# Adding the two halves of an attention output ahead of its transpose, and loading a head pair one step earlier

## The chip, the cores and the metric

The kernel runs on one core of one Trainium2 chip. The metric is the device time of one execution in microseconds (us). The engines of the core are TensorE (PE in the profile; its weight loads are listed apart as PEld), VectorE (DVE), ScalarE (ACT), GpSimd (POOL) and SyncE (SP, which only issues transfers here). They run side by side and each takes its own instructions strictly in order.

## The reference

Three blocks follow one another: attention in which a query sees only the keys that belong to the same of 16 clusters, a mixing layer with a two-layer ReLU network, and a gated network with a convolution of width 3. The change lies in the first block.

```python
def _attn_ref(q, k, v, centroids):          # q, k, v: 2 x 8 x 768 x 64
    ...
    q_assign = np.argmax(np.einsum('bhsd,hcd->bhsc', q_n, c_n), axis=-1)
    k_assign = np.argmax(np.einsum('bhsd,hcd->bhsc', k_n, c_n), axis=-1)
    mask = q_assign[:, :, :, None] == k_assign[:, :, None, :]
    scores = scale * np.matmul(q, k.transpose(0, 1, 3, 2))
    scores = np.where(mask, scores, -1000000000.0)
    scores = scores - np.max(scores, axis=-1, keepdims=True)
    attn = np.exp(scores)
    attn = attn / (np.sum(attn, axis=-1, keepdims=True) + 1e-09)
    return np.matmul(attn, v).astype(np.float32)
```

## The kernel before

Products are made with split operands: a number is kept as a high part, rounded to the format in which TensorE takes it fast, and a low part, the rest. So many tiles come in pairs (`ph`, `pl`; `wh`, `wl`), and the low part is a subtraction on VectorE or GpSimd.

**Tiles and stages of attention.** There are 2 batches of 8 heads; the heads go in 8 pairs, numbered 0 to 7. A head's 768 queries are 6 tiles of 128, so a pair has 12 steps (`s` = 0 to 11) and attention 96 (`n`). The function `step(n)` writes out by hand what each engine does in what order; three tiles of queries are one half of a head, numbered `g`. Within `step(n)` stand, in this order:

- `s_mm(n + 2)`: the scores `sc` of the tile two steps on, two products over `ab` and two over `cd` (which carries the cluster mask), into one of two score buffers.
- `pv_mm(g, r)`: four products of the transposed weights `ph` and `pl` with the values `vt`. After three steps the accumulator `pv` holds, for 384 queries, 64 rows of output from the values' high part and, in the other 64 partitions, 64 rows from their low part.
- `fin_t(g - 1)` (lines 340 to 345, in steps 1, 4, 7 and 10): three transposes of the finished half, `at`.
- `sims` of the next pair, in step 2: 12 small products that give the cluster similarities `sim`.
- `t_mm(n)`: six transposes `tr` of the exponentials, in two halves of three.
- `t_hi(n - 1)` on ScalarE and `t_lo(n - 1)` on VectorE: `ph` and `pl` from `tr`.
- `s_exp(n + 1)` on ScalarE, the exponential `e`, and `s_max(n + 2)` on VectorE, the row maximum of the next scores.
- `fin_a(g)` (lines 335 to 338, in steps 0, 3, 6 and 9): ScalarE copies the accumulator to `asb`, which frees it for the next half's `pv`.
- `fin_x(g - 1)` (lines 347 to 361, in the steps of `fin_t`): ScalarE copies `at` to `ats`, GpSimd adds the two 64-column halves and multiplies each of the three tiles by the reciprocal row sum `rs` into the result `X`.
- `prep(n)` (lines 543 to 575): work for the next pair. `load_raw` asks for the rows `rq` and `rk` on SP's queue, `load_ops` for the operands `ab` and `cd` of one head on GpSimd's queue, `split_ops` makes two subtractions on GpSimd from them, `load_v` the values; VectorE builds the one-hot cluster rows (`mx`, `eq`, `m`, `oh`) from `sim` in steps 2 to 5, TensorE transposes them (`oht`) in step 7, ScalarE makes `os` of them and SP writes them into `cd`. Every second step also moves a job on that fetches and splits weights of the later blocks (`wb`, `wx`, `wh`, `wl`).

**Buffers.** The accumulator `pv` has one buffer. `tr`, `at`, `sim`, `oht` and the later `mt`, `mu` share the three buffers of `ps_t`; a buffer is free when its reader on ScalarE or VectorE is done. `asb` and `ats` have one buffer each, `rq` and `rk` two, `ab` and `cd` three. After the last pair of attention its outputs are mixed (`mt`, in step 8 of the pair behind, needs `X`), and the two networks follow; nothing in them is touched.

## Time and profile before

| | before |
|---|---|
| median of 3 runs | 689.21 us (688.1 to 692.93) |
| the profiled execution | 691.09 us |
| its span, first to last instruction | 689.3 us |
| mean granted TensorE clock in it | 0.988 |
| attention in it | up to about 290 us |

A profile is one execution, recorded engine by engine. A row of a timeline gives the start in us from the span's start, how long the instruction or the run of like instructions took, engine, line of the kernel, operation, and the tiles as out<-in with partitions x elements; in brackets stands how long the engine was idle just before and whose completion ended that. The chain of work is followed back from the last instruction, at each step to what released it: it shows which engine set the pace, and where.

### The profile page before, as it was taken

To read this page: it belongs to the slowest core of one execution; us is meant where nothing else is said; L and a number is where in the kernel's file an instruction comes from. 1 tells how busy PE (TensorE), PEld (TensorE's weight loads), DVE (VectorE), ACT (ScalarE), POOL (GpSimd) and SP (SyncE) were. 2 spreads that over 40 slices of the span, in tenths; PEclk is the share of its full clock that TensorE was granted. 3 is DMA by queue.
4 is the path that set the end of the run, shared out by engine and by line. 5 is a ranking of instruction groups with operands and counts; after the bars stand their busy time and mean duration, and the time that the engine had idled before them with its cause. 6 is when DMAs were issued, how large, how long until landed. Compare 5 with 4: busy or idle time off the path is not lost.

```text
span 689.3 us, 10463 instructions
## 1 busy us (share of the span) xinstructions
PE 673.5 (98%) x3782; PEld 590.9 (86%) x3782; DVE 444.4 (64%) x825; ACT 372.9 (54%) x744; POOL 300.9 (44%) x391
## 2 busy tenths in 40 slices
PE   8799999999999999999999999999999999999997
PEld 6599899899999998888888888888887788888886
DVE  3688888887988898758731877775247535543400
ACT  3588879787878898424311343332133357753611
POOL 6747666666767632515530333332024643322300
PEclk7799999999999999999999999999999999999999
DMA  8957776776756510202310343442014000000111
GB/s 187 146 124 142 156 146 182 132 180 107 180 93 150 103 63 31 92 32 86 94 37 1 125 137 127 131 140 75 1 45 132 7 0 1 1 32 15 40 53 47
DMA packets 31827, 61.58 MB, mean 89 GB/s; under 512 B 15808, under 2 KB 19008, under 8 KB 31776
## 3 DMA queue, kind: packets, MB, share of 16 engines
q1 hardware_dynamic: 15632, 40.08, 19.3%
q0 software_dynamic: 16144, 20.84, 17.1%
q8 instruction: 30, 0.49, 0.3%
q14 instruction: 21, 0.17, 0.1%
HBM read 56.29 MB, written 3.15 MB: 86 GB/s over the span
## 4 chain that ended last, share of the span: by engine, by line
PE 81%; DVE 10%; ACT 2%; issue 2%; DMA 2%; POOL 1%; SPq 1%; ACTq 0%; DVEq 0%; POOLq 0%
PE g L764 10%; PE pv L328 8%; PE tr L304 7%; PE h L641 6%; PE h L643 6%; PE h L642 6%; PE a L657 5%; PE a L659 5%; PE a L658 5%; PE sc L266 4%; PE sc L277 4%; PE sim L203 3%; PE po L798 3%; PE po L799 3%; PE po L800 3%; DVE pl L317 2%
## 5 line engine op out<-in xcount | busy, mean ns | idle before, releaser
L442 POOL TENSOR_TENSOR wl<-wx,wh 128x512 fp32r<-128x512 f32 x48 | 63.1, 1317 | 113.8 <-ACT wh L441 113.4
L317 DVE TENSOR_TENSOR pl<-tr,ph 128x384 fp32r<-128x384 f32 x192 | 97.8, 549 | 22.4 <-ACT ph L313 21.8
L313 ACT CAST ph<-tr 128x384 fp32r<-128x384 f32 x192 | 83.7, 486 | 24.3 <-PE tr L304 23.7
L283 DVE TENSOR_SCALAR_CACHE_REDUCE e<-sc 128x768 f32<-128x768 f32 x96 | 90.8, 947 | 1.9 <-PE sc L277 1.9
L646 ACT ACTIVATE rh<-h 128x512 fp32r<-128x512 f32 (+1 forms) x52 | 29.3, 564 | 112.0 <-PE h L643 112.0
L295 ACT ACTIVATE e<-sc,nb 128x768 f32<-128x768 f32 x96 | 88.2, 919 | 3.0 <-DVE e L283 2.8
L304 PE MATMUL tr<-identf,e 128*128 128x128 f32 x576 | 84.4, 279 | 4.7 <-DVE pl L317 3.1
L647 DVE SCALAR_TENSOR_TENSOR rl<-h,rh 128x512 fp32r<-128x512 f32 (+1 forms) x52 | 33.7, 648 | 83.2 <-ACT rh L646 83.2
L641 PE MATMUL h<-uh,wh 128*128 128x512 f32 (+1 forms) x208 | 78.1, 376 | 1.6 <-DVE rl L647 1.6
L304 PEld LDWEIGHTS tr<-identf,e 128*128 128x128 f32 x576 | 67.5, 143 | 13.1 <-DVE pl L317 8.3
L657 PE MATMUL a<-rh,wh 128*128 128x512 f32 (+1 forms) x208 | 78.1, 375 | 0.5 <-DVE xa L673 0.5
L658 PE MATMUL a<-rl,wh 128*128 128x512 f32 (+1 forms) x208 | 77.7, 373 | 0.3 <-DVE rl L647 0.3
L659 PE MATMUL a<-rh,wl 128*128 128x512 f32 (+1 forms) x208 | 77.6, 373 | 0.0
L643 PE MATMUL h<-uh,wl 128*128 128x512 f32 (+1 forms) x208 | 77.6, 373 | 0.0
L642 PE MATMUL h<-ul,wh 128*128 128x512 f32 (+1 forms) x208 | 77.6, 373 | 0.0
L328 PE MATMUL pv<-ph,vt 128*128 128x384 f32 x192 | 66.0, 344 | 0.2 <-ACT asb L337 0.2
L328 PE MATMUL pv<-pl,vt 128*128 128x384 f32 x192 | 65.3, 340 | 0.0
L266 PE MATMUL sc<-ab 128*128 128x384 f32 x192 | 58.8, 389 | 2.6 <-ACT e L295 2.1
L441 ACT CAST wh<-wx 128x512 fp32r<-128x512 f32 x48 | 29.8, 620 | 57.6 <-DVE wx L395 57.5
L781 POOL TENSOR_TENSOR h<-h,cv 128x768 f32<-128x768 f32 x16 | 29.6, 1850 | 65.4 <-ACT cv L780 65.4
L391 DVE SCALAR_TENSOR_TENSOR wx<-wb,wx 128x512 int32<-128x512 int32 (+3 forms) x52 | 47.9, 920 | 11.3 <-ACT wb L382 9.3
L277 PE MATMUL sc<-cd 80*128 80x384 f32 x192 | 49.9, 342 | 0.5 <-DVE cd L240 0.5
(129 smaller groups left out, 1468.0 us busy)
## 6 DMA issues: line engine op xcount, KB each, us to landing
raw<-in_w_dram SPq DMA_DIRECT2D x32, 512.0 KB, 3.7
ab<-in_qk_dram POOLq DMA_DIRECT2D x30, 384.0 KB, 5.3
cd<-in_qk_dram POOLq DMA_DIRECT2D x15, 384.0 KB, 6.8
raw<-in_win_dram SPq DMA_DIRECT2D x8, 512.0 KB, 3.7
raw<-in_wout_dram SPq DMA_DIRECT2D x8, 512.0 KB, 3.7
rq<-in_qk_dram SPq DMA_DIRECT2D x8, 384.0 KB, 3.9
rk<-in_qk_dram SPq DMA_DIRECT2D x16, 192.0 KB, 4.4
rv<-in_vv_dram SPq DMA_DIRECT2D x8, 384.0 KB, 5.1
```

Source lines behind the costliest of these rows:

```text
L266: nc.tensor.matmul(ps[:, f, 0:HS], ab[:, 0, c0:c0 + P], ab[:, 1, f * HS:(f + 1) * HS], start=True, stop=False)
L283: nc.vector.tensor_scalar(out=e, in0=ps[:, :, 0:HS], scalar1=-SCALE, scalar2=3e38, op0=ALU.mult, op1=ALU.min, accum_out=nb,)
L295: nc.scalar.activation(e, ps[:, :, 0:HS], AF.Exp, scale=SCALE, bias=nb, accum_out=st["sum", n // 3][:, n % 3:n % 3 + 1])
L304: nc.tensor.transpose(pt[:, k, :], e[:, i, k * P:(k + 1) * P], identf)
L317: nc.vector.tensor_sub(lo, st.pop(("t", n, i)), hi)
L328: nc.tensor.matmul(acc, vt[:, h % 2, k, :], m[:, k].rearrange("p a b -> p (a b)"), start=(k == 0 and i == 0), stop=(k == NT - 1 and i == 1),)
L641: nc.tensor.matmul(ph, wh[:, k, ws], uh[g][:, k, ts], start=(k == 0), stop=False)
L642: nc.tensor.matmul(ph, wh[:, k, ws], ul[g][:, k, ts], start=False, stop=False)
L643: nc.tensor.matmul(ph, wl[:, k, ws], uh[g][:, k, ts], start=False, stop=(k == ND - 1))
L657: nc.tensor.matmul(accs[d][:, 0:n], wh[:, i, ds_], rh, start=(f == 0), stop=False)
L658: nc.tensor.matmul(accs[d][:, 0:n], wh[:, i, ds_], rl, start=False, stop=False)
L659: nc.tensor.matmul(accs[d][:, 0:n], wl[:, i, ds_], rh, start=False, stop=(f == NH - 1))
```

## The change

Four things are done.

1. `fin_a` no longer copies the whole accumulator. Each head has its own 64 partitions of a tile `xm` (0 to 63 for the even head of a pair, 64 to 127 for the odd one). ScalarE copies those of the accumulator there as they lie, and the accumulator's other 64 partitions, shifted by 64, into the same partitions of a tile `xo`; GpSimd adds the two in `xm`. `xm` has one tile for each half of the queries, `xo` is one tile.
2. `fin_t` transposes only behind odd heads, when both heads lie in `xm`: three transposes serve two heads. They stand behind the step's `tr` transposes now, and no longer ahead of them.
3. `fin_x` writes the reciprocals of an even head and leaves; behind an odd head it copies `at` to `ats` and makes one product for three tiles and two heads into `X`.
4. `load_raw` of the pair after next and `load_ops` of its first head are called in step 10 of the current pair, where before they were called in step 0 of the next one. Only the first pair ahead is left as it was. `split_ops` of the first head goes from step 2 to step 1, that of the second head from step 5 to step 7.

```diff
@@ -332,33 +332,48 @@
         if part == 2:
             st.pop(("pt", g))
 
+
+
+    xm = {}
+
     def fin_a(g):
-        asb = a_e.tile([P, HS], F32, tag="asb", name="asb", bufs=1)
-        nc.scalar.copy(asb, st.pop(("pv", g)))
-        st["asb", g] = asb
+        _, h, t0 = head_of(3 * g)
+        j, half = h % 2, t0 // 3
+        if j == 0:
+            xm[half] = a_e.tile([P, HS], F32, tag=f"xm{half}", name="xm", bufs=1)
+        x = xm[half][j * D:(j + 1) * D]
+        other = a_e.tile([P, HS], F32, tag="xo", name="xo", bufs=1)[j * D:(j + 1) * D]
+        acc = st.pop(("pv", g))
+        nc.scalar.copy(x, acc[j * D:(j + 1) * D])
+        nc.scalar.copy(other, acc[(1 - j) * D:(2 - j) * D])
+        nc.gpsimd.tensor_add(x, x, other)
 
     def fin_t(g):
-        asb = st.pop(("asb", g))
+        _, h, t0 = head_of(3 * g)
+        if h % 2 == 0:
+            return
         pt = ps_t.tile([P, 3, 2, D], F32, tag="t", name="at")
         for t in range(3):
-            nc.tensor.transpose(pt[:, t].rearrange("p a d -> p (a d)"), asb[:, t * P:(t + 1) * P], identf)
+            nc.tensor.transpose(pt[:, t].rearrange("p a d -> p (a d)"), xm[t0 // 3][:, t * P:(t + 1) * P], identf)
         st["at", g] = pt
 
     def fin_x(g):
         b, h, t0 = head_of(3 * g)
+        j, half = h % 2, t0 // 3
+        if j == 0:
+            st["rs", half] = a_s.tile([P, 3, 2, 1], F32, tag="rs", name="rs")
+        rs = st["rs", half]
+        nc.vector.reciprocal(rs[:, :, j, 0], st.pop(("sum", g)))
+        if j == 0:
+            return
         at = a_e.tile([P, 3, 2, D], F32, tag="ats", name="ats", bufs=1)
         nc.scalar.copy(at, st.pop(("at", g)))
-        sm = st.pop(("sum", g))
-        rs = a_s.tile([P, 3, 1], F32, tag="rs", name="rs")
-        nc.vector.reciprocal(rs[:, :, 0], sm)
-        nc.gpsimd.tensor_add(at[:, :, 0], at[:, :, 0], at[:, :, 1])
-        if h == 0 and t0 == 0:
+        if h == 1 and t0 == 0:
             X[b] = xp.tile([P, NT, DM], F32, tag="x", name="x")
-        for i in range(3):
-            nc.gpsimd.tensor_tensor(
-                out=X[b][:, t0 + i, h * D:(h + 1) * D], in0=at[:, i, 0],
-                in1=rs[:, i].to_broadcast([P, D]), op=ALU.mult,
-            )
+        nc.gpsimd.tensor_tensor(
+            out=X[b][:, t0:t0 + 3, (h - 1) * D:(h + 1) * D].rearrange("p t (a d) -> p t a d", a=2), in0=at,
+            in1=rs.to_broadcast([P, 3, 2, D]), op=ALU.mult,
+        )
 
 
 
@@ -549,17 +564,15 @@
             for part, at in enumerate((2, 2, 3, 4, 5)):
                 if s == at and (nxt > 1 or part > 1):
                     sims_onehot(b, p, part)
-            if s == 0:
-                if nxt > 1:
-                    load_raw(b, p)
+            if s == 0 and nxt == 1:
                 load_ops(b, p, 0)
-            elif s == 2:
+            elif s == (2 if nxt == 1 else 1):
                 split_ops(b, p, 0, nc.gpsimd)
             elif s == 3:
                 st["rv"] = load_v(b, p)
             elif s == 4:
                 load_ops(b, p, 1)
-            elif s == 5:
+            elif s == 7:
                 split_ops(b, p, 1, nc.gpsimd)
             elif s == 8:
                 rv, vt = st.pop("rv")
@@ -567,6 +580,9 @@
             if s == 7:
                 onehot_t(b, p)
                 onehot_rows(b, p)
+        if s == 10 and pair + 2 < B * NP:
+            load_raw(*divmod(pair + 2, NP))
+            load_ops(*divmod(pair + 2, NP), 0)
         if n == NQ - 7:
             queue_chunk(1, lambda: wpc)
         if n >= NQ - 7:
@@ -587,15 +603,16 @@
         g, r = divmod(n - 4, 3)
         if 0 <= g < NHALF:
             pv_mm(g, r)
-        if 0 <= g - 1 < NHALF and r == 0:
-            fin_t(g - 1)
-        elif mixing and (s in (0, 8, 9, 11) or pair == B * NP - 1):
+        fin = 0 <= g - 1 < NHALF and r == 0
+        if mixing and not fin and (s in (0, 8, 9, 11) or pair == B * NP - 1):
             mix = mixing.pop(0)
             got = mix[0]()
         if s == 2 and n < NQ and 1 < pair + 1 < B * NP:
             sims(*divmod(pair + 1, NP))
         if 0 <= n < NQ:
             t_mm(n)
+        if fin:
+            fin_t(g - 1)
         if 0 <= n - 1 < NQ:
             for i in range(2):
                 t_hi(n - 1, i)
@@ -609,7 +626,7 @@
             nc.gpsimd.tensor_scalar(out=sm, in0=sm, scalar1=1e-9, scalar2=None, op0=ALU.add)
         if 0 <= g < NHALF and r == 2:
             fin_a(g)
-        if 0 <= g - 1 < NHALF and r == 0:
+        if fin:
             fin_x(g - 1)
         if mix:
             mix[1](got)
```

On TensorE, in step 4 of a pair (before; `pv` is the last product of the half, `at` the finished half's transposes, `tr` the step's own, `sc` the scores two steps on):

```order
L328 MATMUL pv<-pl,vt 128x384
L344 MATMUL at<-identf,asb 128x128 x3
L304 MATMUL tr<-identf,e 128x128 x6
L266 MATMUL sc<-ab 128x384 x2
L277 MATMUL sc<-cd 128x384 x2
```

The same place on TensorE in the changed kernel:

```order
L328 MATMUL pv<-pl,vt 128x384
L304 MATMUL tr<-identf,e 128x128 x6
L357 MATMUL at<-identf,xm 128x128 x3
L266 MATMUL sc<-ab 128x384 x2
L277 MATMUL sc<-cd 128x384 x2
```

`at` has moved behind `tr`, and in steps 7 and 10 it is gone altogether.

On ScalarE, from step 3 of a pair to its step 7 (before; `e` is the exponential, `ph` the high part of `tr`, `os` the one-hot rows):

```order
L337 COPY asb<-pv 128x384
L313 CAST ph<-tr 128x3x128 x2
L295 ACTIVATE e,sum<-sc,nb 128x768
L350 COPY ats<-at 128x384
L313 CAST ph<-tr 128x3x128 x2
L295 ACTIVATE e,sum<-sc,nb 128x768
L313 CAST ph<-tr 128x3x128 x2
L295 ACTIVATE e,sum<-sc,nb 128x768
L337 COPY asb<-pv 128x384
L313 CAST ph<-tr 128x3x128 x2
L295 ACTIVATE e,sum<-sc,nb 128x768
L350 COPY ats<-at 128x384
```

The same steps on ScalarE in the changed kernel:

```order
L347 COPY xm<-pv 64x384
L348 COPY xo<-pv 64x384
L313 CAST ph<-tr 128x3x128 x2
L295 ACTIVATE e,sum<-sc,nb 128x768
L370 COPY ats<-at 128x384
L313 CAST ph<-tr 128x3x128 x2
L295 ACTIVATE e,sum<-sc,nb 128x768
L313 CAST ph<-tr 128x3x128 x2
L295 ACTIVATE e,sum<-sc,nb 128x768
L347 COPY xm<-pv 64x384
L348 COPY xo<-pv 64x384
L313 CAST ph<-tr 128x3x128 x2
```

In steps 3 and 6 a second copy has come in; `ats` stays where it was in step 4 and is gone in step 7.

On GpSimd, from step 0 of a pair to step 4 (before; rows of `ab` and `cd` from the inputs are `load_ops`, L125 is `split_ops`, `vt` is `load_v`, `sum` a small addition to the row sums):

```order
L107 DMA ab<-in_qk_dram 64x1536
L108 DMA ab<-in_qk_dram 64x1536
L109 DMA cd<-in_qk_dram 64x1536
L609 TENSOR_SCALAR sum<-sum 128x3
L354 TENSOR_TENSOR ats<-ats 128x3x64
L358 TENSOR_TENSOR x<-ats,rs 128x64 x3
L125 TENSOR_TENSOR ab<-rq,ab 64x768
L125 TENSOR_TENSOR ab<-rk,ab 64x768
L116 DMA vt<-in_vv_dram 128x6x64 x2
L609 TENSOR_SCALAR sum<-sum 128x3
L354 TENSOR_TENSOR ats<-ats 128x3x64
```

GpSimd in the changed kernel, from step 10 of the pair ahead to the same step 4 (`wl` is a weight job's subtraction):

```order
L107 DMA ab<-in_qk_dram 64x1536
L108 DMA ab<-in_qk_dram 64x1536
L109 DMA cd<-in_qk_dram 64x1536
L457 TENSOR_TENSOR wl_1749<-wx,wh_1748 128x512
L349 TENSOR_TENSOR xm<-xm,xo 64x384
L626 TENSOR_SCALAR sum<-sum 128x3
L373 TENSOR_TENSOR x<-ats,rs 128x3x128
L125 TENSOR_TENSOR ab<-rq,ab 64x768
L125 TENSOR_TENSOR ab<-rk,ab 64x768
L349 TENSOR_TENSOR xm<-xm,xo 64x384
L116 DMA vt<-in_vv_dram 128x6x64 x2
L626 TENSOR_SCALAR sum<-sum 128x3
```

The loads have gone ahead of the add of step 0, and an add stands between `split_ops` of step 1 and the values' load of step 3.

## Rows read from the trace of the kernel before

**Rows 1.** The page's table: busy us (share of the span) xinstructions, by engine.

```profile
PE 673.5 (98%) x3782; PEld 590.9 (86%) x3782; DVE 444.4 (64%) x825; ACT 372.9 (54%) x744; POOL 300.9 (44%) x391
```

**Rows 2.** Pair 5's stretch: length, PE PEld DVE ACT POOL busy, clock, DMA, GB/s.

```profile
178.27:211.10 32.83, 32.68 (x227) 30.33 (x227) 29.32 (x68) 26.76 (x61) 21.49 (x35) 1.00 0.70 153
```

**Rows 3.** Chain of work in order of time, pairs 5, 6: start, us, what.

```profile
189.40 2.61 PE sim L203 x24
...
192.04 0.57 DVE mx L215
...
202.73 0.48 DVE pl L317
...
203.25 1.08 PE tr L304 x6
...
231.18 0.65 PE tr L304 x6
...
233.23 0.66 PE tr L304 x6
...
235.30 0.33 PE at L344 x3
```

**Rows 4.** Groups by line, shape: xcount | busy us, mean ns | idle before.

```profile
L358 POOL TENSOR_TENSOR x<-ats,rs 128x64 f32<-128x64 f32 x96 | 27.5, 315 | 3.0 <-DVE rs L353 0.5
L125 POOL TENSOR_TENSOR ab<-rk,ab 64x768 fp32r<-64x768 f32 x15 | 27.3, 1821 | 1.6 <-POOL ab L125 0.5
...
L354 POOL TENSOR_TENSOR ats<-ats 128x192 f32<-128x192 f32 x32 | 19.9, 623 | 48.8 <-ACT ats L350 48.0
...
L344 PE MATMUL at<-identf,asb 128*128 128x128 f32 x96 | 15.7, 271 | 0.0
...
L337 ACT COPY asb<-pv 128x384 f32<-128x384 f32 x32 | 15.3, 479 | 1.3 <-PE pv L328 0.3
```

**Rows 5.** Timelines of step 7: pair 4 (first row), pair 5; TensorE, ScalarE.

```profile
170.63 0.55 PE L304 MATMUL tr<-identf,e 128*128 128x128 f32 x3 [0.32 <-ACT ats L350]
...
202.65 0.49 PE L344 MATMUL at<-identf,asb 128*128 128x128 f32 x3
...
204.82 0.99 ACT L242 ACTIVATE os<-oht,ohs 64x768 fp32r<-64x768 bf16 x1 [1.09 <-PE oht L232]
```

**Rows 6.** ScalarE copies: 64 partitions (min/median/max ns), then 128 (count | busy, mean).

```profile
L188 ACT CAST cd<-rk x1: 829/829/829, 6.2 to 6.2; 64x768 fp32r<-64x768 f32 x1
...
L787 ACT CAST gh<-h 128x768 fp32r<-128x768 f32 x16 | 13.5, 842 | 1.9 <-POOL h L781 1.9
```

**Rows 7.** Timelines of steps 3 to 5, pair 6: ScalarE, TensorE, weight loads.

```profile
226.81 0.48 ACT L337 COPY asb<-pv 128x384 f32<-128x384 f32 x1
227.19 0.87 ACT L313 CAST ph<-tr 128x384 fp32r<-128x384 f32 x2
...
227.74 0.19 PEld L328 LDWEIGHTS pv<-ph,vt 128*128 128x128 f32 x1
...
228.62 0.49 PE L344 MATMUL at<-identf,asb 128*128 128x128 f32 x3
...
230.34 0.93 ACT L295 ACTIVATE e<-sc,nb 128x768 f32<-128x768 f32 x1
...
231.56 0.30 PEld L266 LDWEIGHTS sc<-ab 128*128 128x128 f32 x2
```

**Rows 8.** Waits in attention, 43 to 290 us: total us, times, longest.

```profile
POOL ab L125 <- DMA ab<-in_qk_dram: 26.0, 6, 4.8
...
DVE mx L215 <- PE sim L203: 10.9, 6, 1.9
...
ACT ats L350 <- POOL vt L566: 0.7, 2, 0.4
```

**Rows 9.** SP's queue in pair 5, behind the `cd` writes of its step 7.

```profile
208.33 0.57 SPq L93 DMA_DIRECT2D rq<-in_qk_dram  x1
```

## Prediction

> **What bounds the kernel now.** I read the busy table first, then the stretch of one head pair, then the chain of work that ended last inside two neighbouring pairs, then single steps engine by engine. The busy table gives TensorE 98% of the span, with 64% for VectorE, 54% for ScalarE and 44% for GpSimd [rows 1]. The part that the change touches is attention, where those shares are different: in the stretch of pair 5, 32.83 us long, TensorE is busy 32.68, VectorE 29.32, ScalarE 26.76 and GpSimd 21.49 [rows 2]. So three engines are near their limit there, and the chain has to tell which one leads in which step.
>
> The chain shows a step's floor on TensorE: from the `tr` at 231.18 to the next at 233.23 are 2.05 us, with six `tr` transposes, two `sc` products over `ab`, two over `cd` and four `pv` products in it; a group of three `at` transposes adds 0.33 [rows 3]. At step 2 the `sim` products take 2.61 us of TensorE, and the chain then passes to VectorE: it runs without a break from 192.04 (`mx`) to `pl` at 202.73, through the one-hot work and the weight words that VectorE does beside the attention, and comes back to TensorE at 203.25 (step 7) [rows 3]. In pair 5, then, VectorE leads from step 2 to step 6 and TensorE from step 7 on; in pair 6 the `tr` at 231.18 (step 5) is back on TensorE already [rows 3]. Work taken from TensorE is worth its time only in TensorE's steps.
>
> **Removed.** `at` goes from 96 transposes to 48: 16 groups of 0.33 us [rows 3, 4], **5.3 us**. The groups that go are those at steps 7 and 10 (even heads); those at steps 1 and 4 stay. Step 7 is where the chain has just come back to TensorE and step 10 lies in TensorE's own stretch, so I count them in full; in a pair where VectorE leads at step 10 as well, it would be less.
>
> At step 7 there is a second gain. `ps_t` has three buffers, and `at` ahead of `tr` takes one of them. In pair 5 both halves of `tr` then wait for the `pl` halves of the step before: the first was ready behind `at`, at 202.65 plus 0.33, and the six took until 1.08 us after 203.25, where 0.66 from 202.98 was possible [rows 3, 5]. In pair 4 the second half waits for the `ats` copy itself (0.32 us of idle weight loads counted, [rows 5]), and pair 1 looks like pair 4. Without `at` only the second half waits, for the first `pl`. I take 0.43 us (1.08 less 0.65) in these three of the seven pairs that have a successor: **1.3 us**. The earlier `oht` also brings `os` forward, for which ScalarE waited 1.09 [rows 5].
>
> **Added on ScalarE.** Where one copy of 128x384 stood (479 ns, 32 times), two of 64x384 stand; the `ats` copies, of the same size, fall from 32 to 16 [rows 4]. No row shows a 64x384 copy from PSUM. By halves it would cost 0.24; by the nearest rows, a copy of 64x768 at 829 ns beside one of 128x768 at 842 [rows 6], rows of partitions cost nothing, and I take 0.48, of which the next instruction waits 0.38 (`asb` 226.81, `ph` 227.19 [rows 7]). [...] The shifted partitions cost nothing either: the 829 ns copy is such a one.
>
> What waits for the second copy is the next `pv`, which needs the accumulator back. `asb` ends at 227.29, and the next `pv` weight load starts at 227.74 [rows 7]: 0.45 of slack against 0.38. I put it at 0; if ScalarE were late already, it would be 0.38 in each of 32 halves, 12 us.
>
> **Added on GpSimd.** 32 adds of 64x384 and 16 products of 128x384 replace 32 adds of 128x192 (623 ns) and 96 products of 128x64 [rows 4]. Between 192 elements at 623 and 768 at 1821 [rows 4] a 384 comes to about 1.02 us: 48 x 1.02 = 49 us against 19.9 + 27.5 = 47.4 [rows 4], the same. But the add is now ahead of `at` on TensorE. The add can start at 227.3 + 0.38 and ends at 228.7; `at`, moved behind `tr`, is due at 228.62 + 0.66 = 229.28 [rows 7]. So it is hidden by 0.5 us, if GpSimd is free. The order rows say it is: the two `split_ops` now stand a step earlier, at step 1, ahead of this add by 3.6 us of work, and step 2 with its `sim` lies between. If that cover were gone, each of the 16 adds would put up to 1.0 us on TensorE.
>
> **Moved.** `at` behind `tr` costs nothing on TensorE itself: the `sim` products of step 2 and the first half of `tr` at step 5 take the buffer that `at` leaves and wait for `ats`, which is copied half a microsecond before they come. But its copy `ats` stands ahead of the same step's `ph` on ScalarE, as before, and now has its data 0.66 us (six `tr`) later. Queued behind it are `ph`, and `exp` behind that; `pl` on VectorE waits for `ph`, and the `sc` product two steps on waits for `exp` to free one of two score buffers. At step 1 nothing comes of it: the `sim` products follow, and VectorE waits for them anyway (10.9 us in six pairs [rows 8]). At step 4 it does: `exp` at 230.34 ends at 231.27, the `sc` weight load that needs its buffer starts at 231.56 [rows 7]. With `exp` 0.66 later TensorE waits 0.66 - 0.29 = 0.37, in seven pairs: **2.6 us** lost. The bounds: nothing in pairs where VectorE leads (it has `pl` to do meanwhile), the full 0.66 where there is no slack, 4.6 us in all.
>
> **Loads.** SP is not held back by steps: for pair 6 the rows went out at 208.33 straight behind the `cd` writes of step 7, before TensorE's step 10 [rows 9]; asking for them at step 10 of the pair ahead changes nothing. The operand loads go out two steps earlier on GpSimd; GpSimd's wait for them (26.0 us in six places [rows 8]) is a wait of an engine with a third of its time free, and it stands mostly ahead of the second head's split, whose load is not moved. I cost both at 0. What a late split cost elsewhere, `ats` waiting for GpSimd to leave its buffer, was 0.7 us in all [rows 8] and on ScalarE.
>
> **Sum**: 5.3 + 1.3 - 2.6 = 4.0, less 0.2 for places where the slack for `pv` is under 0.38: **3.8 us**. The profiled execution took 691.1 us around its span of 689.3, 1.9 above the median of the runs, 689.2. From the profiled time the sum gives 687.3; from the median **685.4**, which I predict.
>
> **Rivals.** *The whole gain arrives*: the lateness at step 4 is hidden everywhere as it is in pair 5, where VectorE works on without a gap. Then 5.3 + 1.3 = 6.6 and 682.6. For it: VectorE's stretch reaches past step 4 in pair 5. Against: in pair 6 it doesn't.
>
> *Nothing arrives*, since VectorE, not TensorE, sets the length of a pair. It is busy 29.32 us of 32.83 in pair 5 and waits about 1.8 for `sim` [rows 2, 8]: 31.1, and nothing is taken from it. The pair without the 0.66 and 0.43 would be 31.7, and a new gap of 0.66 in `pl` at step 4 lifts VectorE's 31.1 to 31.8. If its other gaps, 1.7 us in that pair, stay where they are, the pair is as long as before: 689.2. [...]
>
> *Slower*: ScalarE becomes the engine that everything waits for. The place is `ats` at steps 1 and 4. If the 0.66 arrives whole in 16 places, 10.6 us, against 6.6 gained, and the second copy takes a little of the `pv` slack, the time is 689.2 + 4.0 = 693.2 or more. It decides from 6.6/16 = 0.41 us of loss for each remaining `at`. For it: the two slacks seen, 0.45 and 0.29, are both under 0.66. Against: ScalarE is busy 26.76 of pair 5's 32.83 us [rows 2], and step 1 is covered by `sim`.
>
> **How the numbers follow.** Forecast (684 to 687.4) 0.47; whole gain or better (under 684) 0.19; nothing (687.4 to 691) 0.22; slower (over 691) 0.12. A measurement of this kernel can tell about 1%, here 6.9 us, from no change. Faster by over 1% means under 682.3, which takes more than half of the whole-gain case: 0.12. Slower by over 1% is half of the slower case: 0.06. The rest, 0.82, is the same. The range leaves out about 0.1 on each side: 682 to 691.5; the likeliest case's own is 684 to 687.4.
>
> **What would show it.** Steps 7 and 10 shorter by 0.33 us, step 7 more where it was long; `tr` at step 7 without its wait for the second `pl`; `ats` at steps 1 and 4 about 0.66 later against its `pv`; a wait of `sc` for `exp` at step 4's end; copies of 64x384 at 0.48; GpSimd as busy as now; no wait of `at` for GpSimd. It is wrong if `at` waits for the add, if `pv` waits for `xo`, or if VectorE's idle time in a pair grows by what TensorE saved.

## The result, and the profile after

The changed kernel takes **700.18 us** (median of 6 runs, 699.5 to 703.15), the kernel before 689.62 beside it: a ratio of 1.0145, 95% interval 1.0124 to 1.0165. It is 10.6 us slower, where 3.8 less was forecast. The profiled execution took 699.5 us around a span of 697.7. Of the ten executions of `c2_short_add` below, two lay over 1.5% above its fastest and count neither in its time nor in its ratio.

The page's table after (busy us, share of the span, instructions):

```profile
PE 672.9 (96%) x3734; PEld 582.3 (83%) x3734; DVE 452.3 (65%) x825; ACT 383.5 (55%) x760; POOL 301.4 (43%) x311
```

Beside [rows 1]: TensorE has 48 instructions less and is no less busy; ScalarE has 10.6 us more, of which 64 copies of 0.47 for 32 of 0.48, with 16 `ats` less, make 7.4; the rest, 3.2 us, is about the overlap with the next instruction that it has lost behind `asb` (32 times 0.48 less 0.38, an estimate from [rows 7]; busy time counts an overlap once). GpSimd's time is the same. VectorE has the same 825 instructions and is busy 7.9 us longer. Nothing in the forecast said so, and it turns out to be about half of the answer.

Pair 5's stretch after (length, then PE PEld DVE ACT POOL busy, clock, DMA, GB/s), beside [rows 2]:

```profile
182.32:216.04 33.72, 32.65 (x220) 29.60 (x220) 30.05 (x66) 27.77 (x62) 21.95 (x24) 1.00 0.66 133
```

The pair has grown from 32.83 to 33.72, VectorE in it from 29.32 to 30.05 and ScalarE from 26.76 to 27.77.

For comparisons one row is enough: the stretch from the first `sc` over `cd` for the scores of step 14 to that for step 95, 81 steps, at a granted clock of 1.00. What lies ahead of it differs by some us from one execution to the next (the stretch begins between 50.11 and 55.19 us in the kernels that have one in the table below), so its length says more of a change than a span does. Before, then after:

```profile
53.99:269.67 215.68, 213.34 (x1503) 203.22 (x1502) 185.72 (x416) 178.85 (x409) 137.44 (x221) 1.00 0.60 128
```

```profile
52.92:276.28 223.36, 215.93 (x1463) 197.83 (x1463) 189.99 (x418) 187.58 (x422) 136.82 (x149) 1.00 0.58 122
```

7.7 us of the loss lie in it, with VectorE 4.3 us busier. Waits after in attention (43 to 290 us; total us, times, longest), beside [rows 8]:

```profile
PEld tr L304 <- DVE pl L317: 14.9, 26, 1.8
...
PE tr L304 <- DVE pl L317: 8.4, 14, 1.6
DVE mx L215 <- PE sim L203: 7.3, 6, 1.2
...
PEld sc L266 <- ACT e L295: 4.0, 12, 0.4
...
PEld pv L328 <- ACT xo L348: 2.1, 6, 0.9
PEld at L357 <- issue: 2.0, 9, 0.2
```

In the same 247 us before, `tr` waited 6.5 us (weights) and 1.6 (products) for `pl`; now it is 14.9 and 8.4. `sc` waits 4.0 us for the exponential (1.2 before) and `pv` 2.1 for `xo` (0.4 for `asb` before), both of which the prediction had named as signs.

The groups that are new (count | busy us, mean ns | idle before):

```profile
L349 POOL TENSOR_TENSOR xm<-xm,xo 64x384 f32<-64x384 f32 x32 | 32.6, 1018 | 71.9 <-ACT xo L348 71.8
...
L348 ACT COPY xo<-pv 64x384 f32<-64x384 f32 x32 | 15.2, 474 | 0.8
L347 ACT COPY xm<-pv 64x384 f32<-64x384 f32 x32 | 15.2, 474 | 0.7 <-PE pv L328 0.2
...
L373 POOL TENSOR_TENSOR x<-ats,rs 128x384 f32<-128x384 f32 x16 | 14.2, 886 | 13.8 <-ACT ats L370 11.9 <-DVE rs L366 1.5
```

The durations are those forecast from [rows 4] and [rows 6] (0.48 and 1.02; the product came at 0.89). So none of the new instructions was dearer than thought; what failed is what they do to their neighbours. ScalarE in steps 3 and 4 of pair 6, beside [rows 7]:

```profile
231.17 0.48 ACT L347 COPY xm<-pv 64x384 f32<-64x384 f32 x1
231.67 0.47 ACT L348 COPY xo<-pv 64x384 f32<-64x384 f32 x1
232.17 0.86 ACT L313 CAST ph<-tr 128x384 fp32r<-128x384 f32 x2
...
234.46 0.48 ACT L370 COPY ats<-at 128x384 f32<-128x384 f32 x1 [0.54 <-PE at L357]
```

and TensorE's weight loads where step 4 ends:

```profile
236.65 0.30 PEld L266 LDWEIGHTS sc<-ab 128*128 128x128 f32 x2 [0.37 <-ACT e L295]
```

From `xm` to `xo` are 0.50 us and from `xo` to `ph` again 0.50: each copy is over before the next instruction begins. Before, `ph` came 0.38 after `asb`, while it was still running. And `sc` waits 0.37 there for the exponential, the number of the prediction for this place.

### The profile page after: what moved, and what is told of

The parts are those of the page before. It is cut to its first block, busy times and chain, and to the rows that moved or that the text cites. A ratio compares the mean times of both kernels' runs of the same rounds, so it can differ in the third digit from the quotient of the medians.

```text
span 697.7 us, 10305 instructions
## 1 busy us (share of the span) xinstructions
PE 672.9 (96%) x3734; PEld 582.3 (83%) x3734; DVE 452.3 (65%) x825; ACT 383.5 (55%) x760; POOL 301.4 (43%) x311
## 4 chain that ended last, share of the span: by engine, by line
PE 71%; DVE 14%; ACT 7%; issue 4%; DMA 2%; POOL 1%; SPq 1%; ACTq 0%; DVEq 0%; POOLq 0%
PE g L781 10%; PE h L658 5%; PE h L660 5%; PE h L659 5%; PE a L675 5%; PE a L674 5%; PE a L676 5%; PE pv L328 5%; PE tr L304 5%; DVE pl L317 4%; PE po L815 3%; PE po L817 3%; PE po L816 3%; PE sc L266 3%; PE sim L203 3%
## 5 line engine op out<-in xcount | busy, mean ns | idle before, releaser
L304 PE MATMUL tr<-identf,e 128*128 128x128 f32 x576 | 86.0, 279 | 9.9 <-DVE pl L317 9.5
L349 POOL TENSOR_TENSOR xm<-xm,xo 64x384 f32<-64x384 f32 x32 | 32.6, 1018 | 71.9 <-ACT xo L348 71.8
L406 DVE SCALAR_TENSOR_TENSOR wx<-wb,wx 128x512 int32<-128x512 int32 (+3 forms) x52 | 51.3, 987 | 11.4 <-ACT wb L397 9.4
```

The lines of the kernel that those rows point to most:

```text
L304: nc.tensor.transpose(pt[:, k, :], e[:, i, k * P:(k + 1) * P], identf)
```

## The experiments

| run | us | ratio to before, 95% interval | stretch, us | VectorE in it |
|---|---|---|---|---|
| before | 689.6 to 692.0 | 1 | 215.68 | 185.72 |
| after | 700.18 | 1.0145 (1.0124 to 1.0165) | 223.36 | 189.99 |
| a1_start0 | 694.92 | 1.0073 (1.0052 to 1.0095) | 219.70 | 190.05 |
| a2_one_copy | 694.28 | 1.0064 (1.0041 to 1.0086) | 219.27 | 190.74 |
| a3_at_ahead | 700.02 | 1.0141 (1.0111 to 1.0171) | 223.68 | 191.63 |
| a4_loads_back | 701.44 | 1.0157 (1.0128 to 1.0187) | 224.74 | 190.39 |
| c1_one_copy_ahead | 691.34 | 1.0009 (0.9982 to 1.0036) | 217.48 | 191.53 |
| c2_short_add | 688.63 | 0.9984 (0.9956 to 1.0012) | | |
| c3_extra_add | 698.45 | 1.0113 (1.0081 to 1.0146) | 222.67 | 192.99 |
| b1_loads_only | 693.31 | 1.0036 (1.0012 to 1.0060) | 217.84 | 187.92 |
| b2_fold | 703.43 | 1.0184 (1.0159 to 1.0208) | 226.90 | 190.13 |
| y1_before_reduce | 702.92 | 1.0184 (1.0146 to 1.0223) | 216.39 | 185.22 |
| y2_one_copy_reduce | 698.18 | 1.0102 (1.0079 to 1.0125) | 212.29 | 185.86 |
| y3_after_reduce | 707.47 | 1.0229 (1.0190 to 1.0268) | 220.70 | 187.33 |
| z0_before_words | 688.20 | 0.9948 (0.9925 to 0.9971) | 214.53 | 184.27 |
| z1_words_moved | 689.32 | 0.9974 (0.9954 to 0.9994) | 214.08 | 188.65 |
| z3_after_words | 698.70 | 1.0131 (1.0107 to 1.0156) | 221.75 | 186.06 |
| d1, d2 (shift) | 747.92, 746.92 | 1.0813, 1.0797 (each ± 0.004) | | |
| d3_shift_first | 705.78 | 1.0231 (1.0200 to 1.0262) | | |

**The second copy.** The first theory was that the two copies hold ScalarE up because they start at different partitions; the rival, that the late `at` does all of it. Two runs take the shift away in two ways, and a third puts `at` back.

```diff
 a1_start0: both copies read and write partitions 0 to 63
-        x = xm[half][j * D:(j + 1) * D]
+        x = xm[half][0:D]
+        if j == 0:
+            nc.gpsimd.memset(xm[half][D:2 * D], 0.0)
 ...
-        nc.scalar.copy(x, acc[j * D:(j + 1) * D])
-        nc.scalar.copy(other, acc[(1 - j) * D:(2 - j) * D])
+        nc.scalar.copy(x, acc[0:D])
+        nc.scalar.copy(other, acc[0:D])
 a2_one_copy: one copy of the accumulator
 ...
+        nc.scalar.copy(asb, acc)
+        other = asb[j * D:(j + 1) * D]
+        nc.gpsimd.tensor_add(x, other, other)
 a3_at_ahead: fin_t(g - 1) ahead of t_mm(n), all else as changed
```

> Two copies as in the change, but both read and write partitions 0 to 63, for both heads, and the add lies there too (so the odd head is not put beside the even one and the low half is not added). Theory A, the copies hold ScalarE up because they start on other partitions than their neighbours: in the changed kernel the step from the first copy to the second and from the second to ph is 0.50 us each, against 0.376 from asb to ph before. Here both fall to about 0.38, ScalarE gets 0.25 us back in each of 32 halves, and the time comes down to 686 to 692. Theory B, the late at and ats behind tr: the steps between the copies may shorten, but the time stays within 2 us of 700.

> One copy of 128x384 as before, and the add of GpSimd, of the same size, takes its 64 partitions from that copy twice (so the high part is added to itself and not to the low one). Everything else as in the change. Theory A (ScalarE's second copy is the loss): 684 to 688, which is what the sum of the prediction gives with the copy taken out. Theory B (at and ats too late): 696 to 700, no better for having one copy less.

> The change with at ahead of tr again, in steps 1 and 4, and nothing else undone. Theory B: ats has its data early again, ph is no longer held up behind it, the time falls by 4 us or more, to 690 to 696. Theory A: no gain; at now waits on TensorE for GpSimd's add, which ends 0.6 us after at would start, in 16 places, so 700 to 708.

a1 and a2 gave back 5.3 and 5.9 us, less than the first theory alone wanted (686 to 692 and 684 to 688) and more than the second allowed, and a3 nothing. ScalarE in a1, step 3 of pair 6:

```profile
227.66 0.48 ACT L349 COPY xm<-pv 64x384 f32<-64x384 f32 x1
228.04 0.47 ACT L350 COPY xo<-pv 64x384 f32<-64x384 f32 x1
228.41 0.86 ACT L313 CAST ph<-tr 128x384 fp32r<-128x384 f32 x2
```

The same two copies, as long as in the changed kernel, now follow each other at 0.38 and 0.37. So the wait of the next one went with the change of the start partition, and it costs 0.25 us for each two copies (1.00 less 0.75). In two places of the changed kernel `xo` of an even head, which reads the accumulator from partition 64 on and writes from 0 on, is followed by an operation that reads SBUF and not PSUM (`v`, `wb`), and there the distance is 0.38 again. Behind `xo` of an odd head, which writes from 64 on, `wb` comes after 0.50, and so does `wh` in another place. Whether the start that is read counts only against an earlier one in the same memory isn't settled by these four places. As a2, with one copy less, gains only 0.6 us over a1, the number of copies hardly counts; a1's clearing of the unused half on GpSimd makes this comparison rough.

In a3 the wait of `sc` is halved, but another has come (43 to 290 us):

```profile
PEld at L357 <- POOL xm L349: 6.3, 13, 0.8
...
PEld sc L266 <- ACT e L295: 2.0, 6, 0.4
```

`at` now waits for GpSimd's add, which the late place had hidden. With two slow copies both places of `at` cost the same.

**One copy and `at` ahead together**, and the add cut short:

```diff
 c1_one_copy_ahead: a2 and a3 together
 c2_short_add: c1, and
-            nc.gpsimd.tensor_add(x, other, other)
+            nc.gpsimd.tensor_add(x[:, 0:D], other[:, 0:D], other[:, 0:D])
```

> The changed kernel with both edits that the earlier runs tried apart: ScalarE makes one 128x384 copy instead of two 64x384 copies (GpSimd adds the half at hand to itself, the low half is left out of the sum), and `at` stands ahead of `tr` again, as in the kernel before. Theory 1, separate prices (the second copy 5 to 6 us, the late `at` 3.2 us in step 5, the second of them hidden with two copies because `at` then waited for GpSimd's add): with one copy the add ends about half a us earlier, `at` waits little for it, and the time is 690 to 692.5 us. Theory 2, `at` waits for GpSimd's add here too and the place doesn't matter: 694 to 696 us.

> The kernel of the run before in this list, with GpSimd's add cut from 384 to 64 columns, some 0.3 us instead of 1.01 (five sixths of the sum are left out; those columns of `xm` stay zero). Theory 1, GpSimd's adds lengthen VectorE's work that runs beside them or keep `at` waiting: VectorE's busy time falls by 4 us or more towards that of the kernel before (444 us) and the time is 687 to 689.5 us. Theory 2, the adds cost the other engines nothing: within 1 us of the run before in this list.

c1 came as expected, 2.9 us under a2: the late `at` costs that, once the copy is out of its way (2.6 was forecast). But c1 is only level with the kernel before, though it has 48 transposes less and no second copy. Its stretch:

```profile
52.99:270.47 217.48, 210.53 (x1463) 198.94 (x1463) 191.53 (x418) 174.29 (x395) 131.92 (x149) 1.00 0.61 127
```

TensorE works 2.8 us less than before, ScalarE 4.6 less, and VectorE 5.8 us more, and the stretch is 1.8 longer. The saved transposes are there all the same. Step 7 of all pairs, before, after and in a2 (sum over 7 places; step 10 follows in words):

```profile
sum 22.40, PE 21.85 PEld 18.90 DVE 17.62 ACT 15.87 POOL 3.15; mean PE 3.12 PEld 2.70 DVE 2.52 ACT 2.27 POOL 0.45
```

```profile
sum 21.81, PE 19.53 PEld 16.32 DVE 19.76 ACT 16.31 POOL 11.97; mean PE 2.79 PEld 2.33 DVE 2.82 ACT 2.33 POOL 1.71
```

```profile
sum 19.10, PE 18.92 PEld 16.51 DVE 17.91 ACT 12.85 POOL 8.85; mean PE 2.70 PEld 2.36 DVE 2.56 ACT 1.84 POOL 1.26
```

Step 7 is worth 3.3 us with one copy and 0.6 with two; step 10 went from 14.37 to 12.49 with one and to 14.02 with two. c2, with the add at a sixth, has a median 2.7 us under c1's and in the range of its first theory, but the runs of either spread over 7 us (686 to 694) and the intervals of the two ratios overlap: what the length of the add is worth stays open.

**VectorE and GpSimd.** A direct look: the kernel before, with an add more on GpSimd, for which only the next `asb` can wait.

```diff
 c3_extra_add: before, in fin_a
+        nc.gpsimd.tensor_add(spare[0:D], asb[0:D], asb[0:D])
```

> The kernel before with one GpSimd add more for each half, 64 partitions by 384 columns on the copy `asb`, into a tile that nothing reads (32 adds, 1.01 us each by the changed kernel's rows). Nothing waits for it but GpSimd's own next work and the next `asb`. Theory 1, GpSimd's work lengthens VectorE's beside it: VectorE's busy time rises by 4 us or more over 444 us and the time is 692 to 696 us. Theory 2, only late GpSimd work counts and no such collision: 689.5 to 691 us with VectorE's busy time within 2 us of 444.

It cost 7.8 us, more than the 692 to 696 of the first theory, and its stretch is 7.0 longer with VectorE 7.3 us busier; `asb` waited for the extra add for 1.4 us in two places:

```profile
53.62:276.29 222.67, 215.96 (x1502) 203.05 (x1502) 192.99 (x416) 179.50 (x408) 159.74 (x247) 1.00 0.58 124
```

One word of a weight job in step 3 of pair 2 shows how, in the kernel before and in c3 on VectorE, then c3's GpSimd at that time:

```profile
95.49 0.54 DVE L391 SCALAR_TENSOR_TENSOR wx<-wb,wx 96x384 int32<-96x384 int32 x1
```

```profile
95.98 1.88 DVE L393 SCALAR_TENSOR_TENSOR wx<-wb,wx 96x384 int32<-96x384 int32 x1
```

```profile
95.61 1.83 POOL L125 TENSOR_TENSOR ab<-rk,ab 64x768 fp32r<-64x768 f32 x1
97.63 0.91 POOL L340 TENSOR_TENSOR spare<-asb 64x384 f32<-64x384 f32 x1 [0.18 <-ACT asb L337]
```

The extra add stands ahead of the operand loads, and the split (`ab`) came 1.9 us later for it, the word only 0.5; so the same word began 0.37 us behind the split's start and ended 0.42 us after its end at 97.44, as if it had stood still until GpSimd was done. Over the stretch the words take VectorE 17.8 us instead of 11.7 and the rows of `eq`, `m` and `oh` 14.8 instead of 13.5, together all of its 7.3 more. Every operation that was seen to grow like this (`wx`, the word above; `eq` times `iota`, a mean of 0.59 us in c3 for 0.35; `oh`, up to 2.16 for 0.55 in the kernel before) works from SBUF to SBUF; `pl`, which reads PSUM, has a mean of 0.547 us over its 192 places in c3 (0.549 before), and the row maximum (`e` on VectorE) and `mx` keep their mean of 0.94 and 0.56. Why such an operation isn't over until GpSimd's is, no run shows; measured are the times, 0.54 us in the kernel before and 1.88 beside the split of 1.83.

So the next runs take the words' wait away, to see whether the gain comes. In three kernels each word operation is replaced by one of about the same length with one input (a mean of 0.54 us for 384 columns and 0.68 for 512 in each of the three).

```diff
 y1 (before), y2 (c1), y3 (changed)
-        nc.vector.scalar_tensor_tensor(out=j["x"], in0=j["b"].bitcast(I32), scalar=3, in1=j["x"], ...)
+        nc.vector.tensor_reduce(out=j["x"], in_=j["b"], axis=AX.X, op=ALU.max)
 ...
-        j["put"](j["x"].bitcast(F32))
+        j["put"](j["b"])
```

> The kernel before, with each of VectorE's three operations on a weight job (`wx`, over the tile in SBUF, two inputs in two of them) replaced by a maximum over the columns of `wb`, one input, of the same length (0.55 us for 384 columns by the rows of `mx` and `m`); the words of the weights are left out, `wh` and `wl` are made from `wb`. VectorE has as much work as before, but in these places none that was seen to grow long beside GpSimd. Theory 1, VectorE's `wx` wait for GpSimd's instruction to end: VectorE's busy time falls by about 5 us, the time by 0 to 3: 687 to 690.5 us. Theory 2, no such wait: 689.5 to 691.5 us with VectorE's busy time as before.

> The kernel with one copy and `at` ahead of `tr` (the low half left out of the sum), with the same replacement of `wx`. Theory 1, the saved transposes arrived there and were given back where VectorE's `wx` waited for GpSimd's adds and products at their new times: 682 to 686 us, 4 to 7 us under the first run of this list. Theory 2, something else took the gain: within 1.5 us of the first run of this list, as the two kernels were without the replacement (691.3 and 690.7).

> The changed kernel with the same replacement of `wx`. Theory 1, of its 10.6 us of loss some 5 are VectorE's waits for GpSimd: 692 to 696 us, 3 to 7 us over the first run of this list. Theory 2, none of it is: 9 to 12 us over the first run of this list.

The differences came as the first theory wanted them: y2 is 4.7 us under y1, y3 4.6 over it. The times themselves lie some 12 us over the ranges, all three alike, and the reason lies behind attention: with `wl` made from `wb`, the next job's `wb` waits for GpSimd's `wl`, a wait that is new, in the later blocks 48.5 us in 27 places in y1. In the stretch, which ends ahead of that, y1 is like the kernel before, in VectorE's time too (its first theory wanted 5 us less), and y2 is shorter:

```profile
54.45:270.84 216.39, 213.39 (x1503) 203.33 (x1502) 185.22 (x416) 178.95 (x408) 134.88 (x221) 1.00 0.60 128
```

```profile
52.63:264.92 212.29, 209.20 (x1463) 198.94 (x1463) 185.86 (x416) 173.95 (x396) 129.53 (x149) 1.00 0.62 130
```

With VectorE at 185 to 186 us in both, the stretch falls by 4.1 us from y1 to y2 (3.4 from the kernel before) and TensorE's work by 4.2: the missing transposes arrive. Steps 7 and 10 give 5.2 of it, and the other steps together take 1.1 back. In c1 VectorE has 5.8 us more, and 5.8 less 4.1 is the 1.7 by which its stretch is longer (1.8 in the rows).

**The loads.** The prediction costed them at 0.

```diff
 a4_loads_back: changed kernel, load_raw, load_ops, split_ops where they were
 b1_loads_only: kernel before, these three where the change puts them
```

> The change with the loads and the two splits where they were before (loads in step 0 of the pair ahead, splits in steps 2 and 5). If the moved loads matter for themselves or add to the loss: 690 to 698. If they only clear GpSimd for the add: the split of step 2, 3.6 us, now stands ahead of the add of step 3, at in step 4 waits for GpSimd for 1 to 3 us in seven pairs, 705 to 715. If neither: 700, within 1.

> The kernel before with the moved loads and splits alone (rows and first operands asked for in step 10 of the pair ahead, splits in steps 1 and 7). Theory 1, the moved loads do nothing to TensorE and the splits meet no VectorE work that they hold up: 689.5 to 691 us. Theory 2, a split of 1.82 us at its new place holds up VectorE's `wx` or one-hot work: 692 to 695 us.

b1 is 2.9 us slower by itself, as its second theory had it, 2.2 of it in the stretch, and VectorE is 2.2 us busier there. A word in its pair 3:

```profile
145.43 1.49 DVE L387 TENSOR_SCALAR wx<-raw 128x512 int32<-128x512 int32 x1
```

A split had begun at 144.75 and took 1.83, to 146.58; the word ends 0.34 behind it. In a4 the splits stand where they were and meet the words together with the new adds (a word of 2.16 us at 94.41 beside a split from 94.33 on), so nothing is won back: a4 is 1.3 us over the changed kernel, within the intervals, and closest to "neither" of its three cases.

**Words at other steps.** If the wait is a matter of place, moving the words should help, and more so where the adds are.

```diff
 z0 (before), z1 (c1), z3 (changed)
-        elif n % 2 == 0:
+        elif s in (1, 4, 5, 6, 10, 11):
             pump(THIN)
```

> The kernel before, a weight job's six stages at steps 1, 4, 5, 6, 10 and 11 of a pair instead of the even steps, all else as it was. Theory 1, moving the words pays only where GpSimd's add stood beside them: 689.5 to 692 us here (GpSimd has `ats` at the ends of steps 1, 4 and 10 in this kernel). Theory 2, the new steps are better in any case: 687 to 689 us.

> The kernel with one copy and `at` ahead of `tr` (the low half left out of the sum), all its weight words whole, but a job's six stages stand at steps 1, 4, 5, 6, 10 and 11 of a pair instead of at the six even steps; at the ends of these steps GpSimd was mostly idle in the trace of that kernel, at the ends of steps 0, 2 and 8 it was in an add, a split or the values. Theory 1, VectorE's words wait for GpSimd's instruction: VectorE's busy time falls by 3 us or more from 451.7, and the time from 691.3 to 685.5 to 689 us. Theory 2, this wait is not what holds the gain back: 690 to 693 us.

> The changed kernel, whole, with a weight job's six stages at steps 1, 4, 5, 6, 10 and 11 of a pair. Theory 1, the change added VectorE waits for GpSimd where the words stood (steps 0, 2 and 8): 694 to 697.5 us, 3 us or more under the changed kernel's 700.2 and so more than the words' place is worth in one comparison by itself. Theory 2, the words' place is worth the same here as in the kernel before (0.5%) or less: 697.5 to 700 us.

By the ratios, z0 gained 0.5%, z1 0.35% over c1 and z3 0.14% over the changed kernel, the last two within their intervals: so the second theory of z0 and of z3 holds, the words' place is worth no more where the adds are, and z1 lies 0.3 us outside the range of its first theory. That doesn't go against the y runs, since the wait moved on: in z1 the words take VectorE 11.3 us in the stretch (16.2 in c1, 11.8 in z0), but the rows of `eq`, `m` and `oh` take 17.3 (15.4 and 12.1), and VectorE as a whole is still 4.4 us over z0 (188.65 and 184.27); 4.4 less 4.1 is 0.3, and the stretches differ by 0.5 the other way. z0 is the one kernel with the whole sum that was faster than before: 688.20 us beside 691.99, ratio 0.9948 (0.9925 to 0.9971).

**Can a whole kernel have the gain?** Two ways were tried. b2 adds the halves on TensorE.

```diff
 b2_fold: before, in fin_t; fold is two identities of 64, one above the other
-            nc.tensor.transpose(pt[:, t].rearrange("p a d -> p (a d)"), asb[:, t * P:(t + 1) * P], identf)
+            nc.tensor.matmul(pt[:, t], asb[:, t * P:(t + 1) * P], fold, start=True, stop=True)
```

> The kernel before, with the halves added on TensorE: `at` is made by a matmul of `asb` with two identities of 64 stacked on top of each other (128 rows, 64 columns), so that it comes out with the halves added, 128x3x64 instead of 128x3x2x64. GpSimd's add goes, its three products become one, the copy `ats` is half as long. Order and places are those of the kernel before. Theory 1, TensorE's stream is half as long for `at` (64 columns instead of 128, 96 times) and ScalarE's and GpSimd's work shrinks: 686 to 689 us. Theory 2, a matmul in float32 with a moving matrix that isn't an identity takes as long as the transposition or longer, weights included: 689.5 to 692 us.

Its `at` (count: minimum, median, maximum ns; first and last start):

```profile
L347 PEld LDWEIGHTS at<-fold,asb x192: 187/192/192, 41.1 to 299.4; 128*128 128x128 f32 x192
L347 PE MATMUL at<-fold,asb x192: 217/275/275, 41.3 to 299.5; 128*128 128x64 f32 x192
```

A float32 product ran as two, each with a weight load of 192 ns; the 96 transposes had one of 139 each, and of `pv`, whose operands are rounded, the four products of a step are four instructions in the same trace, started 0.18 us apart. A group of `at` takes 0.61 us to the next `tr` instead of 0.33, which in 32 groups is 9 of the 12.8 us lost (an estimate); VectorE is 4.4 us busier in the stretch here too. The second theory was right, and too mild.

d1 to d3 make one copy and shift the other half by a transfer on SP's queue:

```diff
 d1_shift: before, in fin_a; GpSimd adds xo to asb a step later, `at` in steps 4 and 5
+        nc.sync.dma_start(out=xo, in_=asb[(1 - j) * D:(2 - j) * D])
 ...
 d2_shift_later: rows asked for in step 10, adds three steps later, `at` in steps 4 and 7
 d3_shift_first: d2, adds one step earlier, ahead of split_ops
```

> A kernel with the whole sum. Loads and splits as in the kernel before; ScalarE makes one 128x384 copy of the accumulator (`asb`), SP's queue shifts its other 64 partitions into `xo`, GpSimd adds the two into `xm` one step later, and the transposes for two heads stand ahead of `tr` in step 4 (first half of the queries) and step 5 (second half) of the next pair; the last pair goes the old way, so that the end of attention is not put off. Theory 1, without the second copy and the late `at` the gain of 48 transposes less arrives, less what GpSimd's adds at their new place hold up VectorE: 685 to 689 us. Theory 2, `ats` in steps 4 and 5 one behind the other makes ScalarE late, or the adds hold up VectorE as in the run with an extra add (698): 691 to 698 us.

> A kernel with the whole sum, as the first one with a shifted half, but: the next pair's rows are asked for in step 10 of the pair ahead, so that they don't stand behind the shift on SP's queue; GpSimd adds a whole half (three steps) later, with two tiles each for `asb` and `xo`; the transposes for two heads stand in steps 4 and 7, the outputs of a pair are mixed from step 9 on; weight words at steps 1, 4, 5, 6, 10 and 11. Theory 1, the gain arrives: 684 to 688 us. Theory 2, the transposes at step 7 bring back the wait for the buffers of `tr` there (3.3 us), or the shifts delay the operand loads: 689 to 695 us.

> The second kernel with a shifted half (whole sum), with GpSimd's add one step earlier, ahead of the step's split and not behind it, so that no add waits for a split that waits for operands. Theory 1, this chain alone cost the 55 us, and with it gone the gain arrives: 684 to 689 us. Theory 2, GpSimd's adds still wait for the shifts to land (3 to 6 us beside the operand loads) and `at` for them: 692 to 730 us.

d1 and d2 lost 57 and 55 us, and their waits say where it began, first d1's, then d2's:

```profile
POOL xm L355 <- DMA xo<-asb: 35.5, 9, 6.6
...
PE sim L203 <- DMA rq<-in_qk_dram: 22.1, 6, 5.9
```

```profile
POOL ab L125 <- DMA ab<-in_qk_dram: 57.1, 12, 6.9
...
PE at L361 <- POOL xm L355: 39.1, 6, 9.2
```

In d1 the next pair's rows stood behind the shift on SP's queue (the shift was issued at 263.83 and its add began at 270.43; the rows were asked for at 264.38 and their split began at 272.29); in d2 the add stood behind a split that waited for operands (4.73 us to 116.44, the add at 120.18), and `at` behind that. The granted clock fell as well. TensorE's `sim` waited for rows six times in d1, 5.9 us at the longest, and this is d1 from 152 to 156 us, behind the gap that ended at 147.3, at a granted clock of 0.50 (columns as in the stretches above):

```profile
152.00:156.00 4.00, 4.00 (x19) 4.00 (x19) 2.11 (x5) 1.29 (x3) 0.00 (x0) 0.50 0.00 0
```

Over the whole stretch the clock was 0.88 in d1 and 0.90 in d2, over the whole profiled execution 0.942 and 0.952, where the kernel before had 0.985 to 0.992 beside them. How much of the 57 and 55 us is the waits and how much the clock isn't separated here. d3 takes the two chains away and gets to 705.78, with the clock at 0.99 in its stretch: GpSimd still waits 38.1 us in 8 places for shifts. Whether some other order has the gain stays open.

## Why the prediction was wrong

Each price is the difference of two kernels, the last one a difference of two differences:

| step (us) | forecast | measured in the stretch | by the medians |
|---|---|---|---|
| transposes that go (all) | -6.6 | -4.1 (y1 to y2) | -4.7 |
| `at` behind `tr` | +2.6 | +1.8 (c1 to a2) | +2.9 |
| the second copy, shifted | 0 to +0.2 | +4.1 (a2 to after) | +5.9 |
| GpSimd's new work and splits against VectorE | 0 | +5.9 | +5.4 |
| sum | -3.8 | +7.7 | +9.5, of 10.6 |

The fourth row is what is between c1 and before (+1.8 and +0.7) when the first is taken out. So the rows add up to the distance between the two kernels by the way they are taken, and that they do is no proof of them. The first row holds all of the change that is left in y2, not the transposes alone.

**Right.** The transposes: steps 7 and 10 give 5.2 us with one copy, where 5.6 were forecast for these 13 of the 16 places (4.3 and 1.3). The late `at`, its chain (`ats`, `ph`, exponential, `sc`) and its size. The durations of the new copies and adds, and GpSimd's sum of work. `at` hidden from the add by its late place: the 1.1 and 0.5 us that it waits are few, and a3 shows what it is without it.

**Wrong, "Added on ScalarE".** The step took 0.48 us a copy "of which the next instruction waits 0.38", from `asb` and `ph` [rows 7], and added that "the shifted partitions cost nothing either: the 829 ns copy is such a one" [rows 6]. That row gave the duration of a lone cast; it could not say whether the instruction behind it overlaps. With 0.50 and 0.50 the two copies hold up the next by 1.00 instead of 0.76, and `pv` waits, since `xo` ends 0.50 later behind the copies' start than `asb` did (0.50 and 0.47 against 0.48), over the slack of 0.45, and `ph` begins 0.62 later. The prediction's own bound for that, 0.38 in each of 32 halves, 12 us, was too high; 4 to 6 came. In step 10 the saved transposes gave back almost nothing with two copies because ScalarE was late: `pl` waits 1.5 us there for `ph` and `sc` 0.9 for the exponential. In step 7 it is the words for the larger part: they take 4.1 us of VectorE there (1.7 before), and in y3, with one-input operations in their place, step 7 falls from 21.81 to 19.78 us.

**Wrong, "Added on GpSimd" and "Loads".** Both were costed by GpSimd's own time and by who waits for its results. On that the prediction was nearly right, and c3 shows that it isn't enough: an add for which no engine but ScalarE waits, 1.4 us in all, costs 0.24 us each. What matters is what VectorE does at that moment. The adds, the product and the splits all moved in time, and with them the places where words and one-hot work meet GpSimd. The trace of the kernel before had a place that shows it, in a group of eight `oh` (minimum, median, maximum ns) and a GpSimd row:

```profile
L226 DVE TENSOR_TENSOR oh<-eq,m x8: 546/553/2162, 12.2 to 231.9; 128x384 bf16<-128x384 bf16 x8
...
134.31 1.32 POOL L442 TENSOR_TENSOR wl<-wx,wh 128x512 fp32r<-128x512 f32 x1
```

The long `oh` began at 133.90, while GpSimd was issuing a load, and ended 0.43 us behind this `wl`. The sign that the prediction named, "if VectorE's idle time in a pair grows", is only half of what came: in the stretch its idle time grew by 3.4 us and its busy time, of which no sign spoke, by 4.3.

**The rivals.** "Nothing arrives, since VectorE sets the length" is what c1 did, for another reason than the one given: the rival had VectorE's gaps stay as they are, but in c1 they fell from 30.0 to 26.0 us in the stretch, and VectorE got 5.8 us more to do. "Slower, ScalarE becomes the bound" had the right sign and the right engine for some 4 to 6 us of the 10.6, by the copies and not by `ats` alone. Together they were given 0.34, and slower by over 1% 0.06: the two were held to be alternatives, and they add.

**Open.** VectorE's growth in the changed kernel is 4.3 us in the stretch, not 5.8 as in c1, so the fourth price isn't the same with two copies: y3 is 2.7 under the changed kernel's stretch, and from y1 to y3 the rest of the change costs 4.3, which leaves 3.4 of the 7.7 to the words. The prices overlap. The medians add up to 9.5 and not 10.6 because the kernel before took 690.65 beside c1 and 689.62 beside the changed kernel. Some 2 to 3 us lie outside the stretch; part of it is at the end of attention, where a weight load of `at` waits 0.9 us for the last add.

## What to carry to other kernels

Before work is put on GpSimd or moved there in time, list what VectorE does at that moment from SBUF to SBUF: in c3 such an operation took 1.88 us for 0.54 beside a GpSimd instruction, while the maxima of y1 to y3, which read SBUF too, took 0.54 for 384 columns in all three; GpSimd's free time is no measure of it. A copy's price is the distance to the next instruction's start (0.38 us behind `asb`, 0.50 behind `xo`, both copies of 0.48), and it has to be read from a row where the partitions change as they will in the new code, not from a row of the same duration. Here three engines were near their limit (TensorE 213 us, VectorE 186, ScalarE 179 of the stretch of 216 before), and a delay on ScalarE (4.1) and one on VectorE (5.9) added; rivals must not be weighed as if only one could come.

## What the runs showed of the hardware that was not expected

- Two ScalarE copies in a row of 0.48 us each, from PSUM, start 0.38 apart when both use the same partitions (a1), and 0.50 when the second reads from another start (the changed kernel).
- A VectorE operation on SBUF of 0.54 us took 1.88 beside a GpSimd instruction of 1.83 (c3), and `pl`, which reads PSUM, kept its mean of 0.55.
- A float32 product of 128x64 ran as two instructions with 192 ns of weight load each (b2), where a transpose of 128x128 was one, with 139.
- A shift of 96 KB between partitions by a transfer held GpSimd for up to 6.6 us when rows and operands were being loaded (d1).
